# Two batches' q and k in 1 KB rows, put into token order by matmuls with strided output, in an attention and Swish MLP kernel

## The chip, the cores and the metric

The kernel runs on one core of a Trainium2 chip. The metric is the time of one execution on the device in microseconds (us), a median over several runs. The engines are PE (matmuls), ACT, DVE, POOL and SP; each works through its own queue in order, and they meet through semaphores. SP issues most transfers, POOL the weights and the output; all transfers run on 16 DMA engines.

## What is computed

Sliding-window attention with a linear bias on the distance, for 8 batches of 8 heads, 576 tokens and 64 columns a head, followed by an MLP whose activation is a Swish with one beta for each hidden column:

```python
batch, n_heads, seq, head_dim = (8, 8, 576, 64)
window = 128
scores = scale * np.matmul(q, k.transpose(0, 1, 3, 2))
slopes = 2.0 ** (-8.0 * (np.arange(H, dtype=np.float32) + 1) / H)
bias = slopes[:, None, None] * (-np.abs(rel).astype(np.float32))[None, :, :]
mask = (rel >= 0) & (rel < window)
scores = np.where(mask, scores + bias[None], -1000000000.0)
...
return np.matmul(attn, v).astype(np.float32)
...
x = np.ascontiguousarray(attn_out.transpose(0, 2, 1, 3)).reshape(B * S, H * D)
h = x @ w_in
g = h * (1.0 / (1.0 + np.exp(-beta * h)))
return (g @ w_out).astype(np.float32)
```

x has 4,608 tokens of 512 columns; w_in is 512 x 2,048 and w_out 2,048 x 512. All inputs and the output are fp32.

## The kernel before

**The work.** A token sees itself and the 127 before it, so a key block of 128 tokens meets two query blocks. A batch has four blocks of 128 tokens and a tail of 64. Scores are taken with the keys on the partitions, so that the exponentials are the stationary operand of the product with v; v has a column of ones beside it, which gives the sum that the result is divided by. The result x is put with its columns on the partitions into `XT`, which holds three groups of 512 tokens. The MLP goes by nine groups of 512 tokens: `Hm` (L535; `HS` is one whole step) makes hidden columns in 16 steps of four matmuls each into one PSUM bank, ACT takes a tanh of it (`sig`, L553) and DVE multiplies (`gT`, L554); `OS` (L563) makes 128 output tokens in four groups of four matmuls (L569), and `store` sends them.

**Three ways through the attention.**
- Batch 0 goes by head pair. `get_pair` (L233) loads a pair's k in two transfers of 256-byte rows, so that a partition holds tokens 128 apart, and its q in one of 1 KB rows: four tokens in a row on one partition. POOL casts both to bf16 (`cast_pair`, L259). `TP` (L288) turns them by eight PE transposes into one bf16 PSUM tile, and DVE copies k (L295) and q (L297); the copy of q puts the tokens of a 32-token stretch in another order (L297-299), and everything made of queries stays in that order. `SP_` (L334) puts a bias and mask table into PSUM by an identity matmul (L345), adds the scores (L356) and takes one exp of the whole (L362); visit A holds key block 0 and part of 1, visit B the rest. `PVP` (L381) multiplies with v, `norm` (L375) divides, and `XP` (L400) multiplies by the permutation `perm`, which both turns x and brings the tokens back into order; ACT copies it to `XT`.
- Batch 1 goes by blocks of 128 tokens. `get` (L222) loads q and k in 256-byte rows (64 fp32 of each head), `cast_qk` (L252) casts, `TB` (L314) turns with PE transposes, `SC` (L443) makes scores of a head pair for half a batch, with four exps of part of a row (L469; the bias enters there) and a mask product on DVE (L473). `PV` (L484) makes x of a block, `X` (L508) turns it.
- Batches 2 to 7 are as batch 1, but q and k are turned by the DMA transpose of `DT` (L429; L433 on SP's queue). From batch 4 on x is turned so too.

The tail of batch 0, 64 tokens, comes later: `TT` (L301), `SCT` (L408, with a table of its own, `tablet`, of L186), then `PV(0, 4, ...)`. Batch 1's tail is one of its blocks.

**What sets the order.** The order of PE, SP and POOL is the order of the program throughout, that of ACT and DVE only in the opening, until the first three steps of the MLP. Lists are written out by hand: the opening, `steps` (batch 1's attention beside group 0's first layer), then `items` (group 1's first layer and group 0's second), over which `spread` lays batch 2 and the start of batch 3. `jobs` and `blocks` give the loads, casts and transposes of a batch ahead of its use.

**Buffers and gates.** `fst` has 13 tiles for loads, `bst` four for bf16 q and k; a cast into `bst` waits until the transposes of the tile four before it are done. Three edges matter here. The first load of batch 1 waits until the first piece of W1 has landed (`after(rows(1, 0)[0], w1[0])`). The first DMA transpose of batch 2 waits for the last piece of W2 (L437-438). And POOL issues the pieces of W1 and W2 between casts. Scores use the PSUM pair `SS`; in the opening the visits B use a second pair, `SX`, which is then given back and makes the two banks of the output's pool, from which batch 1 borrows (`sco`, `pvo`, `hpx`).

Of the kernel before, what the change touches and what calls it, by code (L numbers as in the profile page):

```python
# [19 lines left out]
def kernel(  # L20
# [39 lines left out]
    ktok = const.tile([P, 1], F32, name="ktok")  # L60
# [3 lines left out]
    relt = const.tile([P, 2, 64], F32, name="relt")  # L64
    nat = const.tile([P, P], F32, name="nat")
    perm = const.tile([P, P], BF16, name="perm")
    zeros = const.tile([P, 512], BF16, name="zeros")
    table = const.tile([P, H, 3, P], BF16, name="table")
    tablet = const.tile([P, 2, 2, NP, 64], BF16, name="tablet")
# [37 lines left out]

# [6 lines left out]
    def tail_rel():  # L116
        nc.gpsimd.iota(
            relt[:, 0], pattern=[[1, 64]], base=0, channel_multiplier=-1,
            allow_small_or_imprecise_dtypes=True,
        )  # L120
        nc.gpsimd.affine_select(
            out=relt[:, 0], in_=relt[:, 0], pattern=[[1, 64]], base=0, channel_multiplier=-1,
            compare_op=ALU.is_ge, fill=FAR,
        )
        nc.gpsimd.iota(
            relt[:, 1], pattern=[[1, 64]], base=P, channel_multiplier=-1,
            allow_small_or_imprecise_dtypes=True,
        )
        nc.gpsimd.affine_select(
            out=relt[:, 1], in_=relt[:, 1], pattern=[[-1, 64]], base=-1,  # L130
            channel_multiplier=1, compare_op=ALU.is_ge, fill=FAR,
        )
    def constants():
# [5 lines left out]
        for c in range(4):  # L139
            nc.gpsimd.iota(  # L140
                ktok[32 * c : 32 * c + 32], pattern=[[0, 1]], base=c, channel_multiplier=4,
                allow_small_or_imprecise_dtypes=True,
            )
        nc.gpsimd.iota(
            qtok[:].rearrange("p (c r) -> p c r", c=4), pattern=[[1, 4], [4, 32]], base=0,
            channel_multiplier=-1, allow_small_or_imprecise_dtypes=True,
# [7 lines left out]
        nc.gpsimd.iota(  # L154
            nat[:], pattern=[[1, P]], base=0, channel_multiplier=0,
            allow_small_or_imprecise_dtypes=True,
        )
        tail_rel()
# [7 lines left out]
        for h in range(H):  # L166
            nc.vector.tensor_scalar_mul(table[:, h], rel[:], -slopes[h] / qscale)  # L167
        for i in range(2):
            nc.vector.memset(VS[i][:, :, :, D : D + 1], 1.0)
# [63 lines left out]
    def get_pair(b, p):  # L233
# [3 lines left out]
        for e in range(2):  # L237
# [4 lines left out]
            if e == 0:  # L242
                first = r
# [401 lines left out]
    with tc.manual_schedule(engines={ENG.PE, ENG.SP, ENG.Pool}):  # L645
# [146 lines left out]
        for f in steps:  # L792
            f()
# [52 lines left out]
```

## Time and profile before

| | |
|---|---|
| time, median of 5 runs | 350.98 us (349.92 to 352.89) |
| the profiled execution | 349.0 us, its span 347.3 us |
| PE busy | 320.9 us, 92% of the span |
| ACT, DVE, POOL busy | 210.0, 198.0, 106.6 us |
| granted PE clock, mean | 0.985; in the trace's clock records half from 12.84 to 19.66 us and from 43.55 to 46.97 |
| moved by DMA | 51.79 MB; 147,696 of 155,294 packets under 512 bytes |

The time runs from the start of the execution to its end; the span, from the first to the last instruction of the core, is 1.7 us shorter. "Busy" counts a matmul from its start to its modelled end, and neighbours overlap, so a busy PE isn't a PE at its peak. A row of a group or timeline names the engine, the line, the operation, the tile written and the tiles read, then in brackets how long the engine stood idle and what ended it. `SPq` and `POOLq` are the issue of transfers. The chain of waits is followed back from the last instruction; each row of it is start, duration and what was under way.

Places in the profile, by their rows:

| us | what |
|---|---|
| 4.22 | first cast on POOL |
| 6.44 | first copy of k on DVE |
| 12.44 | issue of W1's first piece; batch 1's first load is issued at 19.32 |
| 24.00 | first matmul of the MLP |
| 46.67 | issue of W2's first piece |
| 65.03 | batch 2's first DMA transpose |
| 76.29 | batch 2's first scores |
| 96.56 and 98.57 | batch 3's first scores, two pairs of matmuls |

### The profile page before, as it was taken

How to read it: one execution, taken by the hardware profiler on the slowest of the kernel's cores; microseconds unless marked ns; L12 is line 12 of the kernel's file. 1: busy time of each engine (PE TensorE's matmuls, PEld its weight loads, DVE VectorE, ACT ScalarE, POOL GpSimd, SP SyncE). 2: the span in 40 equal slices, each digit the busy share in tenths (PEclk: the TensorE clock that was granted, in tenths of full speed). 3: DMA queues.
4: the chain of work that ended last, by engine and by line, in shares of the span. 5: the costliest groups of instructions: out<-in, count | busy, mean ns of one | idle time of the engine just before them, and what ended most of it. 6: DMA issues, size and time to landing. Idle time of an engine off the chain costs nothing.

```text
span 347.3 us, 6177 instructions
## 1 busy us (share of the span) xinstructions
PE 320.9 (92%) x2254; PEld 151.3 (44%) x2254; DVE 198.0 (57%) x439; ACT 210.0 (60%) x419; POOL 106.6 (31%) x195
## 2 busy tenths in 40 slices
PE   7697778997989999997999999999999999999995
PEld 2354344433434444443444444444444444544442
DVE  7646687536745776557547764573487356615500
ACT  2455983459746786576548765764788476436511
POOL 6756290227436323611131434131200100010010
PEclk9789989999999999999999999999999999999999
DMA  7999999999999999982468978899111201220012
GB/s 181 234 210 200 199 201 202 196 189 256 193 234 231 236 211 230 228 162 52 94 134 165 212 146 213 161 226 173 54 23 50 77 30 47 42 87 7 26 71 80
DMA packets 155294, 51.79 MB, mean 149 GB/s; under 512 B 147696, under 2 KB 152832, under 8 KB 155264
## 3 DMA queue, kind: packets, MB, share of 16 engines
q1 hardware_dynamic: 148288, 38.29, 59.1%
q0 software_dynamic: 6944, 13.11, 14.6%
q8 instruction: 17, 0.28, 0.3%
q14 instruction: 13, 0.11, 0.1%
q10 hardware_dynamic: 32, 0.01, 0.0%
HBM read 36.71 MB, written 9.44 MB: 133 GB/s over the span
## 4 chain that ended last, share of the span: by engine, by line
PE 64%; DVE 14%; ACT 10%; DMA 4%; issue 3%; SPq 3%; POOL 0%; POOLq 0%; ACTq 0%
PE ops L569 30%; PE hps L546 26%; ACT pt L469 7%; DVE gT L554 5%; DVE pt L473 4%; PE SS L459 3%; ACT sig L553 2%; SPq L228 2%; DMA fst<-in_k_dram 2%; PE pv L502 1%; DMA qkT<-bst 1%; PE pv L498 1%; DVE xn L378 1%; SPq L433 1%; DVE table L167 1%
## 5 line engine op out<-in xcount | busy, mean ns | idle before, releaser
L546 PE MATMUL hps<-XT,W 128*128 128x512 bf16 x564 | 142.2, 381 | 5.3 <-DVE gT L554 3.6
L569 PE MATMUL ops<-W,gT 128*128 128x512 bf16 x576 | 138.9, 379 | 0.0
L554 DVE SCALAR_TENSOR_TENSOR gT<-sig,hps 128x512 bf16<-128x512 bf16 x141 | 95.4, 683 | 74.2 <-ACT sig L553 73.5
L553 ACT ACTIVATE sig<-hps,beta_h 128x512 bf16<-128x512 f32 x141 | 97.2, 699 | 58.5 <-PE hps L546 54.1
L469 ACT ACTIVATE pt<-SS,bias 128x256 bf16<-128x256 f32 (+1 forms) x208 | 81.7, 486 | 15.6 <-PE SS L459 15.5
L546 PEld LDWEIGHTS <-W 128*128 128x128 bf16 x576 | 51.6, 98 | 62.2 <-issue 11.1
L569 PEld LDWEIGHTS <-gT 128*128 128x128 bf16 x576 | 52.4, 98 | 58.0 <-issue 1.9
L473 DVE TENSOR_TENSOR pt<-pt,mask 128x1024 bf16<-128x1024 bf16 x56 | 44.3, 792 | 31.9 <-ACT pt L469 31.7
L582 POOL DMA_DIRECT2D out_dram<-osb x34 | 18.4, 542 | 135.2 <-ACT osb L575 135.2
L575 ACT ACTIVATE osb<-ops 128x512 f32<-128x512 f32 x36 | 21.6, 601 | 42.8 <-PE ops L569 42.8
L270 POOL CAST vs<-fst 128x512 bf16<-128x512 f32 (+1 forms) x40 | 26.2, 665 | 38.9 <-DMA fst<-in_v_dram 38.7
L256 POOL CAST bst<-fst 128x512 bf16<-128x512 f32 (+1 forms) x36 | 23.3, 647 | 42.4 <-DMA fst<-in_q_dram 24.7
L378 DVE TENSOR_TENSOR xn<-pv,zs 128x256 bf16<-128x256 f32 (+1 forms) x68 | 28.4, 420 | 1.6
L459 PE MATMUL SS<-qkT 64*128 64x256 bf16 (+2 forms) x260 | 21.0, 254 | 7.3 <-ACT pt L469 3.9
L257 POOL CAST bst<-fst 128x512 bf16<-128x512 f32 (+1 forms) x36 | 23.0, 638 | 11.0 <-DMA fst<-in_k_dram 10.5
L459 PEld LDWEIGHTS <-qkT 64*128 64x128 bf16 x280 | 10.6, 95 | 32.5 <-issue 30.1
L502 PE MATMUL pv<-vs,pt 128*128 128x65 bf16 x264 | 23.6, 194 | 0.0
L377 DVE RECIPROCAL zs<-pv 128x4 f32<-128x4 f32 (+1 forms) x74 | 12.8, 176 | 18.5 <-PE pv L502 14.3
L502 PEld LDWEIGHTS <-pt 128*128 128x128 bf16 x280 | 19.2, 98 | 9.2 <-issue 0.5
L498 PEld LDWEIGHTS <-pt 128*128 128x128 bf16 x224 | 17.3, 98 | 5.9
L498 PE MATMUL pv<-vs,pt 128*128 128x65 bf16 x212 | 19.7, 193 | 0.0
L362 ACT ACTIVATE pt<-SS 128x768 bf16<-128x768 f32 x4 | 3.2, 810 | 10.9 <-PE SS L356 10.9
(91 smaller groups left out, 127.7 us busy)
## 6 DMA issues: line engine op xcount, KB each, us to landing
out_dram<-osb POOLq DMA_DIRECT2D x34, 256.0 KB, 3.0
fst<-in_q_dram SPq DMA_DIRECT2D x32, 256.0 KB, 4.7
fst<-in_v_dram SPq DMA_DIRECT2D x32, 256.0 KB, 4.4
fst<-in_k_dram SPq DMA_DIRECT2D x28, 256.0 KB, 4.9
fst<-in_k_dram SPq DMA_DIRECT2D x16, 128.0 KB, 3.4
W<-in_moe_w_in_dram POOLq DMA_DIRECT2D x4, 512.0 KB, 7.6
W<-in_moe_w_out_dram POOLq DMA_DIRECT2D x4, 512.0 KB, 11.0
fst<-in_q_dram SPq DMA_DIRECT2D x8, 128.0 KB, 3.4
```

What stands on the lines that cost most here:

```text
L256: nc.gpsimd.tensor_copy(out=t[0:rows, 0], in_=fs.pop(("q", b, sb))[0:rows])
L270: return nc.gpsimd.tensor_copy(out=VS[b % 2][0:rows, sb, :, 0:D], in_=fs.pop(("v", b, sb))[0:rows])
L378: nc.vector.tensor_tensor(out=xn, in0=pv[0:nq, :, 0:D], in1=zs[0:nq].broadcast_to([nq, 4, D]), op=ALU.mult)
L459: nc.tensor.matmul(o, lhsT=qk[64 * e : 64 * e + 64, 1, p, P * kb : P * kb + P], rhs=qk[64 * e : 64 * e + 64, 0, p, P * kb : P * kb + nq], ...
L469: nc.scalar.activation(out=pt[:, e, cols], in_=sps[e][:, cols], func=ACTF.Exp, scale=qscale, bias=bias[:, half, h : h + 1],)
L473: nc.vector.tensor_tensor(out=pt[:], in0=pt[:], in1=masks[m][:], op=ALU.mult)
L498: nc.tensor.matmul(pv[:, hl, 0 : D + 1], lhsT=weights(b, qb - 1, h, 1), rhs=vs[:, qb - 1, h, 0 : D + 1], start=True, stop=False,)
L502: nc.tensor.matmul(pv[:, hl, 0 : D + 1], lhsT=weights(b, qb, h, 0), rhs=vs[:, qb, h, 0 : D + 1], start=qb == 0, stop=True,)
L546: nc.tensor.matmul(hps[:], lhsT=W1[:, c, bass.ts(j, P)], rhs=XT[:, c, c0 : c0 + TOKG], start=(c == 0), stop=(c == NDM - 1),)
L553: nc.scalar.activation(out=sig[:], in_=hps[:], func=ACTF.Tanh, scale=beta_h[:, j : j + 1])
L554: nc.vector.scalar_tensor_tensor(out=gts[g][:, j, :], in0=sig[:], scalar=1.0, in1=hps[:], op0=ALU.add, op1=ALU.mult)
L569: nc.tensor.matmul(ops_, lhsT=gT[:, j, i * P : i * P + P], rhs=W2[:, j, :], start=(j == 0), stop=(j == NFF - 1),)
```

## The change

Batches 0 and 1 both go by head pair. k is loaded as q is, in 1 KB rows of four tokens. `TP` multiplies with the identity into fp32 PSUM instead of transposing, and each matmul writes every fourth column, so that q and k come out in token order; a tile holds one of the two, DVE copies k, and in batch 0 ACT copies q. With the tokens in order, `perm` and its makers go, `XP` uses plain transposes (ACT and DVE copy in turn), and the tail takes its bias from the large table, so `tablet` and its makers go. Batch 1 uses `SP_`, `PVP`, `XP` and a tail of its own in group 1; `TB` goes. `SX` stays in use until the end of group 0's first layer, for visits B, products with v and four of the steps. In the opening the tables are made in three parts, `constants_next` comes later, and the masks, which batch 2 uses first, go from the opening to behind batch 1's casts on POOL. Loads, casts and weights of batch 1 have a new order. The order of `items` differs in that two groups of the second layer that stood at the end of `steps` now come in `items`.

The diff, cut to its core:

```diff
     def constants():
...
-        tail_rel()
...
-        for h in range(H):
+        tables(0, 2)
+
+    def tables(h0, h1):
+        for h in range(h0, h1):
             nc.vector.tensor_scalar_mul(table[:, h], rel[:], -slopes[h] / qscale)
+
+    def ones():
...
     def get_pair(b, p):
-        f = fst_pool.tile([P, 4, 2, D], F32, name="fst", tag="fst")
-        fs["k", b, "p", p] = f
-        for e in range(2):
-            r = nc.sync.dma_start(
-                out=f[:, :, e, :],
-                in_=k[b, 2 * p + e, 0:FULL, :].rearrange("(n r) d -> r n d", n=4),
-            )
...
+        r = []
+        for what, src in (("k", k), ("q", q)):
+            f = fst_pool.tile([P, 2, 4, D], F32, name="fst", tag="fst")
+            fs[what, b, "p", p] = f
+            r.append(nc.sync.dma_start(
+                out=f[:].rearrange("r h c d -> r h (c d)"),
+                in_=src[b, 2 * p : 2 * p + 2, 0:FULL, :].rearrange("h (r c) d -> r h (c d)", c=4),
+            ))
+        return r[0]
...
     def TP(b, p):
         src = staged.pop((b, "p", p))
-        tps = psum_t.tile([P, 2, 4, P], BF16, name="tps", tag="t")
         for i in (1, 0):
+            tps = psum_t.tile([P, FULL], F32, name="tps", tag="t")
+            tok = tps[:].rearrange("d (r c) -> d c r", c=4)
             for c in range(4):
-                nc.tensor.transpose(out=tps[:, i, c], in_=src[:, i, c], identity=ident[:])
...
+                nc.tensor.matmul(
+                    tok[:, c], lhsT=src[:, i, c], rhs=ident[:], start=True, stop=True)
+            (nc.vector.tensor_copy if b or i else nc.scalar.copy)(
+                out=QK[b % 2][:, i, p, 0:FULL], in_=tps[:])
...
-    def TB(b, sb):
...
-        sps = SX if vis == "B" and b == 0 else SS
+        sps = SX if vis == "B" else SS
...
-    def room(b, wide, shape, name):
-        if b == 0 and wide:
-            return psum_h.tile(shape, F32, name=name + "h", tag="hps")
-        return psum_t.tile(shape, F32, name=name, tag="t")
+    def room(b, shape, i):
+        if b == 0:
+            return psum_h.tile(shape, F32, name="pvh", tag="hps")[:]
+        if i is not None:
+            return SX[:, i, 0 : 4 * 66].rearrange("p (a b) -> p a b", b=66)
+        return psum_t.tile(shape, F32, name="pv", tag="t")[:]
...
     def XP(b, p):
         xn = xns.pop((b, "p", p))
-        xt = room(b, p < 2, [P, 4, P], "xtp")
+        xt = psum_t.tile([P, 4, P], BF16, name="xtp", tag="t")
         for n in range(4):
-            nc.tensor.matmul(xt[:, n, :], lhsT=xn[:, n, :], rhs=perm[:], start=True, stop=True)
-        (nc.vector.tensor_copy if b else nc.scalar.copy)(
+            nc.tensor.transpose(out=xt[:, n, :], in_=xn[:, n, :], identity=ident[:])
+        (nc.vector.tensor_copy if p % 2 else nc.scalar.copy)(
...
     def SCT(b):
         qk = QK[b % 2]
         for e in range(2):
+            t = table[:, e]
+            rhs = bass.AP(tensor=t.tensor, offset=t.offset,
+                          ap=[list(t.ap[0]), [P, 2], [6 * P, NP], [1, 64]])
...
-            if g == 0 and j < 6 and j % 2:
-                hs[g, j] = late["o"].tile([P, DM], F32, name="hpx", tag="ops")
+            if g == 0 and j in (0, 1, 4, 5):
+                hs[g, j] = SX[:, j % 2]
...
             SP_(0, "B", 0)
-            constants_next()
+            tables(2, 4)
+            ones()
...
             SP_(0, "B", 1)
+            tables(4, 8)
...
-            tail_table()
...
             PVP(0, "A", 2)
+            constants_next()
+            SP_(0, "B", 3)
...
-            constants_masks()
-            opening.close()
...
-        after(rows(1, 0)[0], w1[0])
-        for sb in range(1, NQB):
-            rows(1, sb)
-        for sb in range(4):
-            get("v", 1, sb)
-        tail()
-        get("v", 1, 4)
-        for sb in range(3):
-            cast_qk(1, sb)
+        after(get_pair(1, 0), w1[0])
+        for p in range(1, NP):
+            get_pair(1, p)
+        get("v", 1, 0)
+        get("v", 1, 1)
+        tail(0)
+        get("v", 1, 2)
+        get("v", 1, 3)
+        tail(1)
+        cast_pair(1, 0)
+        cast_pair(1, 1)
         w1.append(load_w1(2))
-        cast_qk(1, 3)
+        cast_pair(1, 2)
         w1.append(load_w1(3))
-        cast_qk(1, 4)
-        for sb in range(4):
-            cast_v(1, sb)
-        tail_casts()
+        cast_pair(1, 3)
+        cast_v(1, 0)
+        cast_v(1, 1)
+        tail_casts(0)
         w2.append(load_w2(0))
-        cast_v(1, 4)
-        w2 += [load_w2(n) for n in range(1, 4)]
+        cast_v(1, 2)
+        w2.append(load_w2(1))
+        cast_v(1, 3)
+        w2 += [load_w2(n) for n in range(2, 4)]
+        tail_casts(1)
+        constants_masks()
...
+        steps = [h[2], h[3], R(0), h[4], R(1), h[5], A(0), h[6], R(2), B_(0), A(1), h[7], R(3),
+                 B_(1), A(2), h[8], B_(2), A(3), h[9], B_(3), h[10], VA(0), VA(1), h[11],
+                 VA(2), lambda: TT(0), VA(3), h[12], lambda: SCT(0), VB(0), h[13], VB(1), XO(0),
+                 lambda: PV(0, 4, 0), VB(2), h[14], XO(1), lambda: PV(0, 4, 1), VB(3), XO(2),
+                 h[15], lambda: X(0, 4), XO(3)]
         for f in steps:
             f()
+        opening.close()
...
-        h, o = HG(1), o[2:] + two(1)
-        items = h[:2] + [V(1, 4)] + h[2:3] + [T(1, 4)] + h[3:4]
+        h, o = HG(1), two(0) + OG(0, 2) + OG(0, 3) + two(1)
+        rest = {3: [lambda: TT(1)], 5: [lambda: SCT(1)],
+                6: [lambda: PV(1, 4, 0), lambda: PV(1, 4, 1)], 7: [lambda: X(1, 4)]}
+        items = h[:4]
         for n in range(12):
-            items += [h[4 + n], o[n]]
+            items += [h[4 + n], o[n]] + rest.get(n, [])
```

In `steps`, R is `TP(1, p)`, A and B_ are the visits of `SP_`, VA and VB those of `PVP`, XO is `XP`.

## The prediction

> **What bounds the kernel now.** I read the page's slices first, then windows, then the chain of waits, then PE's timeline where the chain leaves the transfers. "Now" is the kernel before, throughout.
>
> ```profile
> PE   7697778997989999997999999999999999999995
> PEclk9789989999999999999999999999999999999999
> DMA  7999999999999999982468978899111201220012
> ```
>
> A slice is 8.7 us. The DMA engines are full from slice 2 to slice 17, to about 148 us. PE has its gaps in the first 12 slices, and then is full nearly to the end.
>
> ```profile
> core 0: us, PE busy (x) PEld busy (x) DVE busy (x) ACT busy (x) POOL busy (x), PEclk, DMA share, GB/s
> ...
> 15.00:20.00 5.00, 4.00 (x30) 2.05 (x32) 2.10 (x7) 1.83 (x2) 4.57 (x13) 0.53 1.25 206
> ...
> 35.00:40.00 5.00, 4.07 (x38) 1.87 (x37) 3.52 (x6) 5.00 (x14) 0.82 (x1) 1.00 1.24 223
> 40.00:45.00 5.00, 3.45 (x25) 1.58 (x25) 2.87 (x5) 5.00 (x15) 3.33 (x4) 0.86 0.79 173
> ```
>
> While batch 1's attention runs beside the first layer of token group 0, ACT is busy all of 35 to 45 us and PE waits for it. The DMA share drops well under 1 there, in 40 to 45.
>
> ```profile
> 82.93 5.87 DMA fst<-in_k_dram
> 88.79 0.05 issue
> 88.84 0.62 POOL bst L257
> 89.47 2.39 SPq L433
> 91.86 0.04 issue
> 91.91 2.07 DMA fst<-in_q_dram
> 93.98 4.55 DMA qkT<-bst
> 98.57 0.28 PE SS L459 x2
> ```
>
> ```profile
> 98.57 0.28 PE L459 MATMUL SS<-qkT 64*128 64x256 bf16 x2 [1.73 <-DMA qkT<-bst]
> ```
>
> ```profile
> core 0: us, PE busy (x) PEld busy (x) DVE busy (x) ACT busy (x) POOL busy (x), PEclk, DMA share, GB/s
> ...
> 75.00:100.00 25.00, 20.80 (x159) 9.31 (x156) 14.06 (x26) 19.44 (x47) 11.60 (x20) 1.00 1.11 225
> 100.00:125.00 25.00, 24.85 (x192) 11.58 (x189) 16.17 (x37) 17.51 (x39) 11.68 (x20) 1.00 1.14 234
> ```
>
> From 75 to 98.57 the chain is transfers and their issue on SP: batch 3's k, its cast, the transposes on SP's queue; PE waits 1.73 us for the third one. Behind it PE is full (24.85 of 25 us in 100 to 125), and batch 4 has slack: its third transpose is issued at 118.81 and lands about 4.1 later (median of the 30), its first scores start at 130.85. So the forecast is: when do batch 3's first scores (two pairs of matmuls) pass, and what PE work is put behind them.
>
> **Transfers.** In the trace's packet records of SP's queue a 256-byte packet takes 18 ns in the median, one of 1,024 bytes 46 ns. A load of 256 KB is 1,024 packets on 16 engines, 1.15 us; in 1 KB rows 256 packets, 0.74 us. A weight load is 512 packets of 98 ns: 3.14 us. The work up to the third k block of batch 2: batch 0 12.1 (k 4.6, q 2.9, v 4.6), W1 12.6, batch 1 15.6, tail of batch 0 1.7, W2 12.6, three block pairs 6.9: 61.5 us. First data come at 1.9, a landing about 1.1 behind the data: 64.5. The cast of that k ended its wait at 67.26. So only 2.7 us of 67 are holes, and cheaper packets arrive sooner one for one.
>
> The change puts 12 loads (4 of k in batch 0, 8 of batch 1) in 1 KB rows. By medians that saves 12 x 0.41 = 4.9 us, by the mean of the 1 KB packets (56 to 61 ns, waits in them) 12 x 0.22 = 2.6. The Trainium skill (DMA: Bandwidth & Descriptors, Specifications) sets line rate at 512 bytes and more, about 27 GiB/s an engine: 1,024 bytes would take 35 ns and the 12 loads save 7.0. The row decides: 46 ns. I take 4.0, as some wait will stay.
>
> The new order spreads the W2 loads between the v casts. Its first W2 load waits for batch 0's tail casts: by the sum of work near 38 us, now 46.67. So the last W2 load lands near 58, not 65.03, and SP, which stands at batch 2's first transpose until then, isn't held there; its own issues get shorter too (0.50 for a load in 1 KB rows, 1.0 for the two half loads of k, 1.1 for a block). I add 0.7 for that and for the hole at 40 to 45. Transfers of batches 2 and 3 come 4.7 earlier; ends 2.2 and 7. Batch 3's pass is then possible at 98.57 - 4.7 = 93.9.
>
> **PE and the engines that feed it.** Opening: the eight table products (8 x 0.39) hold the first copy of k till 6.44 though its transposes end at 5.65; memsets and biases hold the second pair's (9.96 against 9.17), the tail table (2.15) the third's (15.00 against 14.1): 2.5 us that leave the chain. Six table products then lie behind scores, the constants between visits; if that cover goes they cost their 2 us again. Transposes become fp32 matmuls: DVE's copy of k costs 0.66 instead of 0.41 (nearest rows: 0.585 for ACT's 128x512 fp32 copy, 0.68 for gT), and q's goes to ACT at 0.585, in its queue behind both exps of the pair before (0.81 and 1.02). A pair then takes 2.4 of ACT and about 0.45 of turnaround, 2.85 against 3.35 to 5.2 now (exps at 7.79, 11.14, 16.34, 20.33). POOL loses 1.8 us of iotas ahead of its first cast, which then waits for data only. First-layer matmuls start near 20 instead of 24.00.
>
> Batch 1, 24 to 76 now: 32 exps go (rows of four take 1.57), 12.5 us of ACT; eight of 0.81 or 1.02 come, 7.3, and 1.02 for the tail's: ACT -4.2. DVE loses 8 mask products (5.5) and gains 2 on copies. PE gains 4 x (2x384 + 2x512) columns of table matmuls at 0.42 ns (512 in 0.216), 3.0 us, and about 0.4 for the second tail's, against small savings: +3. Work from the first layer's start to the end of group 0's first layer: 64 matmuls of 0.216, 13.8; 32 transposes of 0.055, 1.8; tables 3.0; scores 1.5 (the two heads of a pair run side by side, as L459's four of 256 in 0.39 show); 56 value matmuls of 0.03, 1.7; XP 0.9; batch 0's tail 1.4: 24.1. The stretch takes 34.8 now, some 12 of it waits, most of them for ACT; I take 4, as ACT would have about 19 us of work in it. It ends near 48.5 (58.8 now). With 12 us of waits again PE would lose 8 of its lead and no more. Its data come in time by the same sum of transfers: W1's third piece near 32, used near 33; batch 1's last v near 42.5, used near 43. Ten more first-layer steps and six second-layer groups at 0.86, 13.8, and 0.7 for the tail: PE stands at batch 2's first scores near 63, now 76.29. Their third transpose (issued 71.91, landed about 76.0 now) is no longer behind the gate and lands near 69. PE waits there some 6 us.
>
> From there to batch 3's first scores: now 96.56 - 76.29 = 20.3. The scores stand closer (pace of ACT: about 2.2 for each of the first four, as now), one first-layer step fewer lies among them and batch 1's tail (0.65) comes in: 21.1. PE is there at 90.1, or at 92.4 if the idle wait halves the clock (the trace's clock records grant half for 6.8 us from 12.84, after less idleness; the paced stretch then loses about 2.3). Both are before 93.9, so transfers still set the pass. Behind it lie two second-layer groups more than now: 2 x 0.86 = 1.73.
>
> Sum: 98.57 - 93.9 = 4.7, less 1.73: 3.0 us. Span 347.3 to 344.3; the profiled execution 349.0 (1.7 around the span) to 346.0; against the median of 350.98, 2.0 above it: **348.0**.
>
> **Strided output.** No row shows a matmul that writes every fourth column. It can't be quicker than now (8 in 0.61, about 0.055 each after the first). The skill (PSUM — Partial Sum Buffer, Specifications) speaks against this change: lines are of 8 bytes, and any output that isn't contiguous slows matmuls significantly, without a figure. Two fp32 fill a line, so I take twice the time, 0.11 (an estimate): 64 x 0.055 = 3.5 us of PE; by the row, nothing. PE's lead over the transfers at batch 3 is 93.9 - 84.1 (63 + 21.1, without the wait) = 9.8, which covers it.
>
> **Edits at nothing.** POOL's masks (3.76) go behind batch 1's tail casts, about 44 to 48, ahead of batch 2's casts, whose data come near 55; first used at 69. If data came sooner they would cost up to 3.8 there. First-layer results in SX, no pool tiles from the output banks, tail table read out of the big one: same sizes. XP as transposes, half on DVE: same 0.585. Batch 2's first scores follow the tail's exp (1.02) in the same bank; the wait for data hides it.
>
> **Added wait.** The staging ring has four tiles: batch 2's fourth cast now waits for PE's transposes of batch 1's tail. Behind it on POOL stand batch 2's v casts, two stores and all casts of batch 3. PE gets there near 59, the data near 66: 7 us of cover.
>
> **Rivals.**
> - Transfers move further (0.20): their advance is 7, for the gate on SP held more than the packets. Then PE sets the pass, at 90.1: 98.57 - 90.1 - 1.73 = 6.7 gained, 344.3. For it: SP's chain runs almost unbroken from 65.03, when the gate opens. Against: DMA share 1.11 in 75 to 100, queues full.
> - Transfers hardly move (0.14): mean packet times and new holes, since W2 waits for v casts; advance 2.2, gain 0.5, 350.5. For it: the means above.
> - Slower (0.11): the strided matmuls cost much more. It decides from 84.1 + 64e = 98.57 - 1.73, e = 0.20, so 0.255 for one (4.6 times). At 0.30: pass at 99.8, 3.0 lost, 354.0. Against: nothing in the trace; for it: the skill's word.
> - The forecast (0.55): 348.0, its own range 346.3 to 349.6.
>
> The range, 344.2 to 350.8, takes in the forecast, most of the first two rivals, and leaves out the slower one. 0.5% (1.75 us) is about what a measurement of this kernel can tell from no change. Faster: the forecast but for its tail and the first rival, 0.76; same 0.13; slower 0.11.
>
> **What would show it.** Right: 1 KB packets near 46 ns; first L481 matmuls near 20; no ACT window at 5.00 in 35 to 45; a PE wait of several us for the transposes at batch 2's first scores near 69, and a second at batch 3's near 94. Wrong: PE busy without waits in 60 to 95 (PE or ACT is the bound, strided matmuls dear); the wait for batch 3 at 97 or later (transfers did not move); batch 2's fourth cast waiting for PE.

## The result and the profile after

The changed kernel takes 348.87 us (median of 23 runs, 347.77 to 352.82), the kernel before 351.43 in the runs beside it (42 runs, 348.28 to 354.77). The medians differ by 2.6 us. The ratio, which leaves out executions over 1.5% above the fastest of their kernel, is 0.9942, 95% interval 0.9924 to 0.996: 0.6%, or 2.0 us. The profiled execution took 348.87, span 347.0. That of before had 349.0 and 347.3, so the two profiles differ by only 0.3 us of span. Both the gain in the medians and the small difference of the profiles need an explanation.

The slices of the page after, in the order of those shown of before:

```profile
PE   8867998987999999997999999999999999999995
...
PEclk9999999999999999999999999999999999999999
DMA  8999999999999997971468988799112201120012
```

PE's gaps in the first slices have shrunk but not gone, and no slice is at a lower clock. The windows that showed ACT as the bound in batch 1's attention, and the stretch up to and behind batch 3's first scores:

```profile
core 0: us, PE busy (x) PEld busy (x) DVE busy (x) ACT busy (x) POOL busy (x), PEclk, DMA share, GB/s
...
35.00:40.00 5.00, 5.00 (x39) 2.87 (x37) 2.99 (x6) 3.51 (x5) 4.14 (x7) 1.00 0.86 139
40.00:45.00 5.00, 5.00 (x41) 1.88 (x41) 1.88 (x3) 4.42 (x6) 3.01 (x6) 1.00 1.16 188
75.00:100.00 25.00, 22.19 (x193) 10.88 (x192) 17.57 (x36) 19.56 (x46) 12.05 (x21) 1.00 1.23 212
100.00:125.00 25.00, 24.25 (x173) 11.00 (x172) 15.20 (x32) 17.39 (x38) 11.14 (x19) 1.00 1.12 228
```

ACT no longer fills 35 to 45 us; PE does. The chain of waits, where it held transfers before:

```profile
72.74 0.43 PE SS L352 x2
73.17 0.36 PE SS L357 x16
73.55 1.03 ACT pc L363
74.63 0.41 PE SS L397 x4
...
77.69 1.47 ACT pt L407 x4
79.19 0.79 DVE pt L411
...
93.84 0.97 PE ops L504 x4
94.81 0.22 PE xt L456 x4
95.03 0.86 PE ops L504 x4
95.89 0.33 PE SS L397 x4
```

There is no DMA row in it: from the opening to batch 3's scores (last row) the chain runs through PE, ACT and DVE. PE's timeline of the same kernel at the points that the prediction named:

```profile
21.07 0.41 PE L331 MATMUL pvh<-vs,pt 128*128 128x65 bf16 x8 [2.48 <-DVE xnp L316]
...
23.13 0.59 PE L481 MATMUL SX<-XT,W 128*128 128x512 bf16 x2
...
27.60 0.38 PE L481 MATMUL SX<-XT,W 128*128 128x512 bf16 x1 [1.50 <-DVE gT L489]
...
74.63 0.39 PE L397 MATMUL SS<-qkT 64*128 64x256 bf16 x4 [1.12 <-ACT pc L363]
...
95.83 0.39 PE L397 MATMUL SS<-qkT 64*128 64x256 bf16 x4
```

The first layer starts at 23.13 (24.00 before), batch 2's scores at 74.63 (76.29), batch 3's at 95.83 without a wait (98.57, behind one). Batch 3's third transpose is issued at 89.81 (93.98). So the transfers came 4.2 us earlier, much as forecast, and by the 4.1 from issue to landing its data was there near 93.9, 1.9 before PE.

From these rows the theory: after the change PE's own order sets the pass, the transfers have about 1.9 us of room, and what holds PE is DVE's order in the opening, a two-bank tile and work that the sum had sized too small. The rivals: the transfers still set the end; the strided output is what costs; the gain is the granted clock's.

### The profile page after: what moved, and what is told of

Its sections match the earlier page's. It is cut to its first block, busy times and chain, and to the rows that moved or that the text cites. A ratio compares the mean times of both kernels' runs of the same rounds, so it can differ in the third digit from the quotient of the medians.

```text
span 347.0 us, 6187 instructions
## 1 busy us (share of the span) xinstructions
PE 324.2 (93%) x2288; PEld 154.8 (45%) x2288; DVE 196.0 (56%) x422; ACT 209.5 (60%) x400; POOL 101.4 (29%) x186
## 4 chain that ended last, share of the span: by engine, by line
PE 73%; ACT 12%; DVE 11%; issue 2%; ACTq 0%
PE ops L504 32%; PE hps L481 27%; ACT pt L407 7%; DVE gT L489 4%; DVE pt L411 4%; ACT sig L488 3%; PE SS L397 3%; PE pv L437 2%; PE pv L433 1%; PE tps L250 1%; PE SS L104 1%; PE SX L481 1%; PE SX L283 1%; DVE xnp L316 1%; DVE table L135 1%
## 5 line engine op out<-in xcount | busy, mean ns | idle before, releaser
L481 PE MATMUL hps<-XT,W 128*128 128x512 bf16 x560 | 139.9, 379 | 5.9 <-DVE gT L489 5.3
L407 ACT ACTIVATE pt<-SS,bias 128x256 bf16<-128x256 f32 (+1 forms) x192 | 75.2, 479 | 13.1 <-PE SS L397 13.1
L411 DVE TENSOR_TENSOR pt<-pt,mask 128x1024 bf16<-128x1024 bf16 x48 | 40.0, 834 | 27.9 <-ACT pt L407 27.9
L226 POOL CAST vs<-fst 128x512 bf16<-128x512 f32 (+1 forms) x40 | 24.3, 619 | 32.3 <-DMA fst<-in_v_dram 30.3
L211 POOL CAST bst<-fst 128x512 bf16<-128x512 f32 (+1 forms) x32 | 20.2, 631 | 39.0 <-DMA fst<-in_q_dram 31.3
L212 POOL CAST bst<-fst 128x512 bf16<-128x512 f32 (+1 forms) x32 | 19.6, 613 | 14.2 <-DMA fst<-in_k_dram 14.2
L397 PE MATMUL SS<-qkT 64*128 64x256 bf16 (+2 forms) x240 | 18.9, 252 | 4.2 <-ACT pt L407 2.8
L437 PE MATMUL pv<-vs,pt 128*128 128x65 bf16 x240 | 21.6, 193 | 0.0
L437 PEld LDWEIGHTS <-pt 128*128 128x128 bf16 x240 | 16.4, 97 | 8.3
L397 PEld LDWEIGHTS <-qkT 64*128 64x128 bf16 x240 | 8.5, 94 | 23.9 <-issue 22.6
L433 PE MATMUL pv<-vs,pt 128*128 128x65 bf16 x192 | 18.0, 193 | 0.0
L433 PEld LDWEIGHTS <-pt 128*128 128x128 bf16 x192 | 15.3, 98 | 5.7
L218 POOL CAST bst<-fst 128x512 bf16<-128x512 f32 x16 | 9.8, 624 | 10.4 <-DMA fst<-in_k_dram 8.9
```

The costliest lines, as they stand in the source:

```text
L226: return nc.gpsimd.tensor_copy(out=VS[b % 2][0:rows, sb, :, 0:D], in_=fs.pop(("v", b, sb))[0:rows])
L397: nc.tensor.matmul(o, lhsT=qk[64 * e : 64 * e + 64, 1, p, P * kb : P * kb + P], rhs=qk[64 * e : 64 * e + 64, 0, p, P * kb : P * kb + nq], ...
L407: nc.scalar.activation(out=pt[:, e, cols], in_=sps[e][:, cols], func=ACTF.Exp, scale=qscale, bias=bias[:, half, h : h + 1],)
L411: nc.vector.tensor_tensor(out=pt[:], in0=pt[:], in1=masks[m][:], op=ALU.mult)
L433: nc.tensor.matmul(pv[:, hl, 0 : D + 1], lhsT=weights(b, qb - 1, h, 1), rhs=vs[:, qb - 1, h, 0 : D + 1], start=True, stop=False,)
L437: nc.tensor.matmul(pv[:, hl, 0 : D + 1], lhsT=weights(b, qb, h, 0), rhs=vs[:, qb, h, 0 : D + 1], start=qb == 0, stop=True,)
```

## Experiments

All start from the changed kernel, with one edit or with several of them together, but for two that start from the kernel before. Each has a ratio to runs of the kernel before beside it, with medians of 351.1 to 351.4. To compare with are the 348.87 and 0.9942 of the changed kernel. The intervals of the single edits touch that of the changed kernel, so their sizes are rough. In the diffs `...` marks what is left out.

**DVE's order in the opening.** The first pair of lines is in constants(); constants_next() keeps its memsets, and its loop over the biases becomes constants_bias(h0, h1).

```diff
-        tables(0, 2)
+        tables(0, 6)
...
-            tables(2, 4)
...
-            tables(4, 8)
+            tables(6, 8)
...
             TP(0, 2)
+            constants_next()
...
             PVP(0, "A", 1)
+            constants_bias(0, 4)
...
             PVP(0, "A", 2)
-            constants_next()
+            constants_bias(4, 8)
```

> All constants are still made, only DVE's order in the opening differs: four table products fill DVE's wait for the first transposes (2.6 us idle there in the changed kernel), the memsets stand behind the third pair's k copy, the biases behind two norms. Theory (after the change PE's order, not the transfers, sets when batch 3's first scores pass; the transfers have only some 1.9 us of room: third transpose issued at 89.8, landed about 93.9, scores at 95.8): the third pair's transposes come 0.6 earlier, the wait of 2.5 us for a norm at 21.1 goes, the first-layer matmuls start near 20.5 instead of 23.1, and batch 3's scores pass near 94, where they wait for the transpose again: 1.9 us less than the changed kernel, about 347.0. Rival 1 (the stretch behind the opening waits for data or for ACT anyway): first layer near 20.5, but batch 2's first scores stay within 0.5 of 74.6, time unchanged near 348.9. Rival 2 (the transfers still set the pass as predicted): no change beyond 0.3 us.

Measured: 347.46 us, ratio 0.9898 (0.9857 to 0.9939). PE's timeline of this kernel:

```profile
19.03 0.41 PE L333 MATMUL pvh<-vs,pt 128*128 128x65 bf16 x8 [0.49 <-DVE xnp L318]
...
21.08 0.59 PE L483 MATMUL SX<-XT,W 128*128 128x512 bf16 x2
...
72.56 0.40 PE L399 MATMUL SS<-qkT 64*128 64x256 bf16 x4 [1.12 <-ACT pc L365]
...
79.35 0.61 PE L399 MATMUL SS<-qkT 64*128 64x256 bf16 x4
...
95.09 0.39 PE L399 MATMUL SS<-qkT 64*128 64x256 bf16 x4
```

The 2.48 for a norm became 0.49, and all of the 2.05 is still there at batch 2's scores (74.63 to 72.56). So nothing between 23 and 74 hides the opening: rival 1 falls, and rival 2 with it. At batch 3's scores only 0.7 is left in this profile. About 0.4 of the 1.3 lost goes with a stretch at half clock, 77.92 to 81.33 (the 0.61 for four matmuls instead of 0.40 shows it; from the third to the fifth scores 4.51 us pass instead of 4.11). The other 0.9 lies behind it, where the chain of waits of this kernel goes through DVE:

```profile
81.63 2.12 DVE pt L413
83.75 0.21 DVE XT L464
84.00 0.29 PE pv L439 x4
```

This product with the mask takes 0.68 us in the changed kernel (at 83.32), where no cast of POOL runs beside it; here four do in part. The time says 1.4 of the expected 1.9.

**Contiguous output of the identity matmuls.**

```diff
-            tok = tps[:].rearrange("d (r c) -> d c r", c=4)
+            tok = tps[:].rearrange("d (c r) -> d c r", c=4)
-                out=QK[b % 2][:, i, p, 0:FULL], in_=tps[:])
+                out=QK[b % 2][:, i, p, 0:FULL].rearrange("d (r c) -> d r c", c=4),
+                in_=tps[:].rearrange("d (c r) -> d r c", c=4))
```

> The change with contiguous PSUM output for the fp32 identity matmuls; the copy behind them reads every 128th column instead. Theory (eight matmuls with strided output take 0.87 to 1.05 us where eight with contiguous output took 0.61): 0.3 to 0.4 us less for each of 8 groups of eight, 1.5 us of it in batch 1 and up to 1.3 in the opening, so PE is at batch 3's scores 1.9 earlier and then waits for the transpose: 347.0 to 347.5. Rival 1 (the stride costs nothing, the fp32 output itself is what takes longer): groups of eight stay at 0.87 or more, time unchanged near 348.9. Rival 2 (the copy pays for the strided read): copies of 0.69 grow to 1 us or more, and the time rises by 1 us or more.

Measured: 347.74, ratio 0.9911 (0.9884 to 0.9938). The groups of the changed kernel, and of this one, with busy time and mean ns behind the bar:

```profile
L250 PE MATMUL tps<-ident,bst 128*128 128x128 bf16 x64 | 9.2, 324 | 0.6 <-DVE beta_h L156 0.4 <-DVE qkT L252 0.3
L252 DVE CAST qkT<-tps 128x512 bf16<-128x512 f32 x12 | 8.2, 687 | 6.2 <-PE tps L250 6.2
```

```profile
L252 DVE CAST qkT<-tps 128x512 bf16<-128x512 f32 x12 | 8.2, 687 | 5.2 <-PE tps L250 5.2
L250 PE MATMUL tps<-ident,bst 128*128 128x128 bf16 x64 | 5.9, 231 | 1.3 <-DVE qkT L252 0.8 <-DVE beta_h L156 0.4
```

The stride costs PE 3.3 us of 64 matmuls, 0.05 each: in the chains eight take 0.87 with it and 0.45 without. DVE reads every 128th column at the same 687 ns. Both rivals fall: the reordering is free in the copy, and not in the matmul. Where the 1.1 us of time arises can't be read from this profile: at 348.90 it is one of the slowest of the ten runs, with a half-clock stretch from 20.71 to 24.12, and batch 3's scores come at 95.69, only 0.1 earlier.

**The 12 loads back in 256-byte packets.** Batch 0's k and batch 1's q and k go into a tile [row, 4, 2, 64], one issue for each of the two heads:

```diff
+            f = fst_pool.tile([P, 4, 2, D], F32, name="fst", tag="fst")
+            for e in range(2):
+                r.append(nc.sync.dma_start(
+                    out=f[:, :, e, :],
+                    in_=src[b, 2 * p + e, 0:FULL, :].rearrange("(r c) d -> r c d", c=4)))
```

> The change with its 12 loads (k of batch 0, q and k of batch 1) in 256-byte packets again, two issues for each, same layout, everything else kept. Theory (PE has about 1.9 us behind the transpose at batch 3's scores): transfers come 4.0 to 5.0 us later, the first 1.9 of it is hidden, batch 3's scores wait for their transpose near 98: 2 to 3 us slower than the changed kernel, near 351.3, which is no better than the kernel before. Rival 1 (the transfers set the end one for one): 4.2 us or more slower, 353. Rival 2 (the gain came from the batch 1 rewrite and the granted clock, transfers have much cover): within 0.5 us of 348.9.

Measured: 354.16, ratio 1.0092 (1.006 to 1.0124). 5.3 us lost where 2 to 3 were expected, and by the number rival 1 stands better. The transposes show why the edit wasn't clean: batch 2's third is issued at 74.92 instead of 65.64, 9.3 later. SP now issues 16 half loads of batch 1 at 0.6 us each from 21.31 to 32.29, and the DMA share is only 0.80 in 20 to 30 (1.13 in the changed kernel), so that SP's issues seem to hold the transfers there, and not the packets alone. PE waits 1.53 us for that transpose, and for none at batch 3's scores. A second try had to move transfers alone.

**Six loads in 256-byte packets, one issue each.** As above for pairs 1 to 3 of batch 1, with `out=f[:]` and `in_=src[...].rearrange("h (r c) d -> r c h d", c=4)`.

> The change with six of batch 1's eight loads (pairs 1 to 3) in 256-byte packets, one issue each, batch 0 and the opening untouched, so that only transfers move: 6 x 0.41 = 2.5 us by the packets' medians. Theory (PE stands about 1.9 us behind the transpose at batch 3's scores, and 2.5 behind the one at batch 2's): all but 0.6 is hidden, 349.2 to 349.6, no wait for a transpose of more than 0.7. Rival 1 (transfers set the end one for one, as the loads put back with two issues suggested, 5.3 lost): 351.4, with a PE wait for a transpose. Rival 2 (the loads of batch 1 gate its own stretch: pairs come late for their casts): PE waits for a cast in 28 to 45, 350 or more.

Measured: 349.51, ratio 0.9952 (0.9926 to 0.9977): 0.6 above the changed kernel, as the theory said. Batch 3's third transpose is issued at 94.81 here. In eight profiles whose transfers are unchanged it lies between 88.76 and 91.71, so it moved by 3 to 6 us. PE waits for no transpose, but this profile, the slowest of the twelve runs, can't tell the room: with two stretches at half clock PE was itself 2.9 later, at 98.72, about when that transpose had landed. It is the time that speaks against rival 1, which asked for 2.5 us more; rival 2 falls, as PE waits for no cast. Why six loads moved the transpose by more than the 2.5 of the packets' medians isn't settled.

**First-layer steps out of the two-bank tile.**

```diff
-            if g == 0 and j in (0, 1, 4, 5):
-                hs[g, j] = SX[:, j % 2]
+            if g == 0 and j in (0, 3):
+                hs[g, j] = SX[:, j // 3]
```

> The change with steps 0 and 3 of group 0's first layer in the two banks of SX, the others in the ring of single banks, instead of steps 0, 1, 4, 5 in SX. Theory (a tile of two banks counts as one, so step 1's last matmul waited 1.5 us for the product of step 0, and step 5's 0.2 for step 4's): these waits go, the first layer's second step ends near 26 instead of 28, batch 3's scores pass 1.0 to 1.7 earlier, near 347.5. Rival (the wait only moves: with two ring banks for steps 1, 2, 4, 5 PE waits for their products instead): waits of the same sum in 25 to 36, time within 0.4 of 348.9.

Measured: 347.50, ratio 0.9908 (0.9877 to 0.9939). The waits for gT in 25 to 36 are 0.42 instead of 1.71 (one of 1.50 at 27.60, one of 0.21 at 32.94), and batch 2's scores come at 73.61. The theory's mechanism holds, and its size within the scatter of the runs.

**These three together.**

> The three edits that each gave 1.1 to 1.4 us on the changed kernel (DVE's order in the opening, contiguous output of the identity matmuls, first-layer steps kept out of the two-bank tile) together. All constants are made, nothing is left out. Theory (room against the transfers is near 1.9 us): capped, batch 3's scores wait for their transpose near 94, time 346.5 to 347.3, about as each edit alone. Rival (what stays is PE's own work and ACT's score chain, and the edits add): 348.9 - 3.9 = 345.0, no wait for a transpose at batch 3's scores.

Measured: 346.40, ratio 0.9866 (0.9829 to 0.9903), the best of the study, equal to the four together below. PE's timeline at batch 2's scores, and batch 3's:

```profile
20.14 0.59 PE L484 MATMUL SX<-XT,W 128*128 128x512 bf16 x2
...
68.89 0.29 PE L400 MATMUL SS<-qkT 64*128 64x256 bf16 x2 [1.12 <-ACT pc L366]
70.03 0.40 PE L400 MATMUL SS<-qkT 64*128 64x256 bf16 x2 [0.85 <-DMA qkT<-bst]
...
93.22 0.39 PE L400 MATMUL SS<-qkT 64*128 64x256 bf16 x4
```

1.1 + 1.4 + 1.4 us of single edits give 2.5, not 3.9: the edits don't add, and the wait for a transpose is back. The theory's cap is there, but its place was wrong: it binds at batch 2's third transpose, not at batch 3's. Nor is it the whole. In this profile PE is 5.7 us earlier at batch 2's scores and 2.6 at batch 3's. Of the 3.1 lost between them, by the distances of the rows, about 0.9 is that wait, some 1.7 the work behind it at half clock (69.86 to 73.28), and 0.8 a mask product on DVE beside POOL's casts (1.98 us), less 0.2 won.

**Batch 1's tail earlier.**

```diff
-        rest = {3: [lambda: TT(1)], 5: [lambda: SCT(1)],
+        rest = {1: [lambda: TT(1)], 3: [lambda: SCT(1)],
```

> The change with the transposes and the scores of batch 1's tail each two places earlier among the layer groups, so that its exp is done before batch 2's first scores need the same bank. Theory (the forecast hid this exp behind a wait for data that isn't there, so it costs its 1.1 us): the wait of 1.12 at batch 2's first scores goes, batch 3's pass near 94.7, time near 347.8. Rival (behind it the ACT-paced train of scores takes the same end, or the place is covered by later waits): unchanged, within 0.3 of 348.9.

Measured: 348.70, ratio 0.994 (0.9909 to 0.997). The wait of 1.12 is gone from the timeline, the time isn't lower by more than can be told. In the profile the 1.1 us is there: from the first step of group 1 to batch 2's scores it takes 16.8 us (61.16 to 77.97) instead of 17.9 (56.73 to 74.63), and from there to batch 3's 21.2 as before. All of this comes 4.4 us late, since 10.2 us at half clock fell between 20 and 35, where this program is the same as the changed kernel. Why the median doesn't show the gain is not shown; the runs had a lower clock, 0.994 against 0.997.

**All four together.**

> All four edits together. Theory (transfers cap it near 94): same as the three together within 0.3 us, 346.5 to 347.3. Rival (edits add): 1.1 below the three together, 343.9 if these give 345.0.

Measured: 346.52, ratio 0.9867 (0.9827 to 0.9907), the same as the three. PE's timeline at batch 2's scores shows what took the place of the ACT wait:

```profile
69.09 0.28 PE L400 MATMUL SS<-qkT 64*128 64x256 bf16 x2 [1.36 <-DMA qkT<-bst]
72.48 0.40 PE L400 MATMUL SS<-qkT 64*128 64x256 bf16 x2 [3.10 <-DMA qkT<-bst]
```

With the first scores 5.5 us earlier, the transfers are the bound again in this profile, the slowest of its six runs. A faster PE order gave about 2.5 us here, and the fourth edit nothing on top.

**The old transfer order put back.** Batch 1's four v loads and casts stand together again, ahead of tail_casts(0) and the lines shown.

```diff
         w2.append(load_w2(0))
-        cast_v(1, 2)
-        w2.append(load_w2(1))
-        cast_v(1, 3)
-        w2 += [load_w2(n) for n in range(2, 4)]
         tail_casts(1)
+        w2 += [load_w2(n) for n in range(1, 4)]
```

> The change with the transfer order of batch 1 and W2 put back: all v blocks of batch 1 ahead of the tails, one piece of W2 behind batch 0's tail casts and the other three behind batch 1's. Theory (the forecast's 0.7 for the new order, and 1.9 us of cover at batch 3's scores): transfers of batches 2 and 3 0.5 to 1.5 later, hidden; time within 0.5 of 348.9. Rival 1 (the new order is what released batch 2's first transpose, by several us): it is issued at 62 or later instead of 58.8, time 350.5 or more. Rival 2 (the new order opened holes, since the loads put back to small rows cost more than the whole change had gained in transfers): transposes of batch 3 issued earlier than 89, time no worse.

Measured: 349.71, ratio 0.9932 (0.9905 to 0.9959). Batch 2's first transpose is issued at 60.58 instead of 58.76, its third at 69.04 instead of 65.64, batch 3's third at 91.83 instead of 89.81; PE waits for none of them. So the order seems worth some 2 us of transfers, under cover. That is one profile, and each of the three lies only just beyond what the eight with unchanged transfers show (57.9 to 60.1, 64.8 to 68.4, 88.8 to 91.7). Both rivals fall; the 0.8 us of the medians lies within the scatter, and the ratio shows no loss.

**The granted clock.** The clock records list stretches at half speed, each of 3.41 us or twice that. Over 90 timed runs, the kernel before has a mean clock of 0.986 and never more than 0.995, and a straight line through them gives 349.6 +- 0.4 us at full clock plus 121 +- 29 for 1 of clock lost. The changed kernel's 23 runs have 0.997 and give 348.5 +- 0.1 plus 222 +- 25. At full clock, where the kernel before has no run, 1.1 us would be left of the 2.4 between 348.87 and the median of these 90 runs, 351.2. That is a correlation, so two tries at the cause.

The clock bears on the experiments above as well. The runs of the three single edits had mean clocks of 0.994 to 0.996, those of the three together 0.991. Brought to the changed kernel's 0.997 by its slope of 222 (an estimate), the single edits give 1.6, 1.9 and 2.1 us and the three together 3.9: each more than measured, and still less than the sum.

The kernel before with idle matmuls in its opening:

```diff
+    def fill_in(n):
+        w = psum_h.tile([P, 512], F32, name="idl", tag="hps")
+        for _ in range(n):
+            nc.tensor.matmul(w[:], lhsT=zeros[:, 0:P], rhs=zeros[:], start=True, stop=True,
+                             skip_group_check=True)
...
             TP(0, 0)
+            fill_in(4)
...
             TP(0, 1)
+            fill_in(6)
...
             betas()
+            fill_in(3)
...
             TP(0, 2)
+            fill_in(5)
...
             TP(0, 3)
+            fill_in(2)
```

> The kernel before with 20 idle matmuls in the opening, in the waits of TensorE for the copies of batch 0, written to a bank nobody reads; nothing is left out. All 22 timed runs of the kernel before, in the comparison with the first experiments, had a mean granted clock of 0.979 to 0.995, while 16 of 23 of the changed kernel had 0.998 or more. Theory (transfers set the end of the kernel before, so the half-clock stretch of 12.84 to 19.66 in its opening lies under cover): the stretch goes and the mean clock rises towards 0.995, the time stays within 0.5 us of the kernel before. Rival (the change won its 2.5 us by the granted clock): 1.7 us less for each half-clock stretch of 3.41 us that goes, 347.5 to 349.5.

Measured: 351.64, ratio 1.0 (0.9967 to 1.0033), mean clock 0.991. This decides nothing: the fillers ahead of the third group delayed it, the scores of that pair came at 20.16 behind a wait of 2.94 for DVE, and the opening was 4.4 us longer. The second try has 3, 5 and 4 fillers behind the first three groups only:

> The kernel before again with idle matmuls in the opening, now only inside waits for copies (3, 5 and 4 behind the first three groups of transposes), none ahead of the third group, where the first try pushed the tail-table products under the mask work and made the opening 4 us longer. 68 timed runs of the kernel before lie on a line of 349.1 us plus 168 us for 1 of mean granted clock lost (their mean clock 0.986, none above 0.995), 23 of the changed kernel on 348.5 plus 222 (mean 0.997). Theory now (most of the change's 2.5 us is waits gone from the opening and from batch 1, which let the clock fall, and only some 0.5 is left at equal clock): mean clock near 0.991, time 0.6 to 1.2 below the kernel before. Rival (the clock only goes along with other things, such as late transfers): clock up, time within 0.3 of the kernel before.

Measured: 350.52, ratio 0.9997 (0.9967 to 1.0027), mean clock 0.991 against 0.985. The median is 0.7 lower, within the theory's range, but the interval holds no change as well. The profile shows where a gain would go:

```profile
22.11 0.59 PE L553 MATMUL hps<-XT,W 128*128 128x512 bf16 x2
...
98.20 0.29 PE L466 MATMUL SS<-qkT 64*128 64x256 bf16 x2 [2.47 <-DMA qkT<-bst]
```

No half-clock stretch falls on the opening here (the first is at 45.72), and the first layer starts 1.9 us earlier than the 24.00 of the kernel before. At batch 3's scores PE is still 1.1 us earlier (95.45 against 96.56), but it waits 2.47 us for the transpose instead of 1.73 and passes at 98.20 instead of 98.57: 0.4 is left. So in this execution the transfers cover most of what PE had gained. Whether the slower executions of the kernel before lose by their clock stays open.

The changed kernel without its 11 idle matmuls (`idle(8)` and three `idle(1)` taken out):

> The change without its eleven idle matmuls (eight ahead of the first data, three between the value blocks of batch 0): only work that computes nothing is left out. Theory (the clock counts: each half-clock stretch of 3.41 us costs about 1 us, as PE is the bound from the opening on): the opening runs at half clock, mean clock 0.985 to 0.99, time 1.5 to 2.5 us above 348.9 although PE has 0.65 us less to do among its own work. Rival (the opening waits for casts and copies, which the clock doesn't touch): clock down, time at 348.9 or up to 0.6 below it.

Measured: 351.50, ratio 0.9995 (0.9971 to 1.0019). The windows of this kernel:

```profile
25.00:30.00 5.00, 2.99 (x11) 1.24 (x10) 1.11 (x2) 0.83 (x2) 5.00 (x9) 0.77 1.26 233
30.00:35.00 5.00, 5.00 (x20) 2.83 (x19) 2.44 (x4) 2.06 (x3) 0.03 (x1) 0.66 1.15 197
```

Taking away work that computes nothing costs 2.6 us, all that the change had won. Its first layer starts at 24.31 (23.13), batch 2's scores come at 78.57 (74.63), batch 3's at 99.75 (95.83). The 3.9 us of delay are complete by 36.88, where the changed kernel is at 32.94. 1.2 of them come in the opening, whose first matmuls take longer (two of 512 columns 1.04 us at 7.45, where the changed kernel's take 0.60); the clock records of this profile begin only at 10.24, so that half clock is read from the durations there. The other 2.7 come with two half-clock stretches, from 23.90 and from 30.72. So the clock does set time in the changed kernel, where PE is the bound; the rival falls.

## Why the prediction was right, and where it was not

The forecast was 348.0; 348.87 came, inside its own range. Part of its mechanism held, but that the number did is in part luck: two errors nearly cancelled.

- **Transfers: right.** 4.7 us earlier was forecast; batch 3's third transpose is 4.2 earlier (3.9 by the means of eight profiles with the new transfers and three with the old), and 1 KB packets take 46 ns in the median. Batch 2's first transpose is issued at 58.76, and its gate was forecast to open near 58. The rivals "move further" and "hardly move" fall. The part for the new order, 0.7, looks too small: put back it moved transposes by 1.8 to 3.4, in one profile.
- **The opening: wrong.** "First-layer matmuls start near 20": 23.13. The step that failed is "2.5 us that leave the chain. Six table products then lie behind scores, the constants between visits". DVE does things in program order: four table products stand ahead of the norm and the betas that the third pair waits for, and memsets and biases ahead of a norm that PE waits for until 21.07. The prediction had priced this case ("if that cover goes they cost their 2 us again"): the first experiment got 2.05 back.
- **Batch 1's stretch: wrong in its terms.** It was to take 24.1 us of work and 4 of waits. In the timeline from 23.9 to 56.7, PE does 29.5 of work and waits 3.3. Table matmuls took 3.9 (3.0 forecast), identity matmuls 3.7 (1.8, with as much again for the stride left to cover), scores 2.4 (1.5), value matmuls 2.1 (1.7), XP 1.5 (0.9), tail 2.2 (1.4). Waits were sized well (4 forecast). With the late opening, the first layer of group 0 ends at 56.7 instead of 48.5.
- **From there to batch 2's scores: too small.** 14.5 us were forecast and 17.9 came. The ten steps and six groups take the 13.8 of the sum; the tail's own work takes 1.2 (0.7), and the waits for gT in two places and for the tail's exp, some 2.9 together, were not in it. So PE is there at 74.63 and not at 63: 3.1 by the opening, 5.1 by batch 1's stretch, 3.4 here. From there to batch 3's scores 21.1 was forecast and 21.2 came.
- **Who sets the pass: wrong.** "PE waits there some 6 us" became 1.12 for the tail's exp, the edit that "the wait for data hides". PE's lead of 9.8 us, which was to cover the strided output and the tail, did not exist. The strided output cost time (1.1 us less without it), and the tail's exp stands in PE's chain, though the runs without that wait were not faster. Hence 95.83 and not 93.9.
- **Strided output: right in size, wrong in its cover.** Twice the time, 0.11 us each, as estimated from the skill (PSUM — Partial Sum Buffer, Specifications), which gives no figure; 0.05 more for each is measured. The slower rival, at 0.255 each, falls.
- **Added wait: didn't show.** POOL's fourth cast of batch 2 waited 0.17 us, for data.
- **Behind the pass:** 1.73 us for two layer groups was forecast; from batch 3's scores to the end it takes 251.2 us instead of 248.7, 2.4 more, of which waits of the first layer for gT are 0.9 (4.5 against 3.6 behind 95 us).

The sum on the profiles: 98.57 - 95.83 = 2.7, less 2.4, is the 0.3 of span that the two profiles show, not 3.0. So the profiled execution lies 2.9 us above the 346.0 that the prediction had for it. The number came right because the prediction put 2.0 us on top for the median of the runs, and for the changed kernel nothing was to be put there: its profiled execution is the median itself. For the kernel before, the profiled execution was one of its lowest times (349.0 against medians of 351.1 to 351.4), and the fastest executions of the two kernels differ by no more than 0.5 us. The other 2 us of gain lie in executions of the kernel before that took longer than the profiled one, by waits that no profile here shows.

Part of the gain goes with the clock, by the two lines 1.3 of 2.4 us. The Trainium skill states the rule of the clock (TensorE: Matmul & The Clock Gate, What's actually happening): a free-running window of 3,413 ns whose activity decides. The records agree in the length of the stretches, 3.41 us. But that the clock is the cause is shown for the changed kernel only; for the kernel before it is argued from a correlation. And it doesn't say why the profiled execution of the kernel before lies so low: that one had a clock of 0.985, and the 35 runs at 0.984 to 0.986 have a median of 351.4. About their lines the runs of the kernel before scatter by 1.1 us, those of the changed kernel by 0.5. A kernel whose pass is set by transfers would scatter so, since their place moves by some 3 us between profiles with the same transfers; that is argued, not shown. Nor does any run take the new form of batch 1 apart from the loads, so what each part of the change is worth stays open too.

## What to carry to other kernels

A wait that ends last in a profile says how much room the next bound leaves only if that bound is summed with measured spacings of its own instructions; here PE was 1.9 us behind the transfers, not 9.8 ahead, and costs put under that cover came to stand in PE's own chain. Where two bounds were within 2 us, single edits on one of them did not add: test them together before counting. And before a sum made on one profile is moved to a median, ask where that profile lies among the runs, and at which clock: between runs of the same program a clock of 0.99 instead of 1.00 went with some 2 us here.

## What the hardware showed that was not expected

- A reordering is free where DVE reads PSUM (687 ns for 128x512 fp32 with either order) and costs PE twice the spacing where a matmul writes every fourth column (0.87 against 0.45 us for eight).
- Half-clock stretches within one execution start at multiples of 3.41 us from each other: 12.84 and 43.56 in the kernel before (9 times), 21.14 and 79.17 with the steps out of the two-bank tile (17 times). Their place differs between executions of programs that are the same up to there: the profile of the changed kernel has none, that of the earlier tail has 10.2 us of them before 35, and its first step of group 1 comes 4.4 us later.
- DVE's mask products take longer beside POOL's casts. Of the 48 mask products in the changed kernel's profile, the 24 with no cast of POOL beside them take 0.67 to 0.69 us, the others up to 2.17, and the more the longer the two overlap (correlation 0.95). In the first try with fillers, DVE's eight tail-table products took 4.38 us beside POOL's mask work; in the profile of before, apart from it, 2.15. No run changed POOL's work alone to test it.
